# Attention and a two-layer FFN in one kernel: late attention visits at other places, the last tiles prepared earlier, and the last tile projected in two halves

## The chip, the core and the metric

The kernel runs on one core of a Trainium2 chip. The metric is the device time of one execution in microseconds (us); less is better. Engines are named as the profile names them: PE (TensorE, matmuls), PEld (its weight loads), DVE (VectorE), ACT (ScalarE), POOL (GpSimd) and SP (SyncE, which issues DMAs here).

## The reference

Local attention with a few global keys and a linear distance bias, then an FFN without biases:

```python
scores = scale * q @ k^T + bias          # (4, 8, 768, 64), bias = -slope_h * distance
keep   = (pos_k < n_global) | (0 <= rel < n_local)          # 8 and 96
a      = exp(where(keep, scores, -1e9) - max); a /= sum(a) + 1e-9
x      = (a @ v) as 3072 x 512
h      = x @ w_in                        # 512 x 2048
out    = max(0.01 * h, h) @ w_out        # 2048 x 512
```

## The kernel before

The 3072 rows of x are 24 steps of 128 rows. A step has two units of attention (four heads each), 48 in all. Attention is computed in the band alone, and at the end of it a flag tells whether that was allowed. The FFN runs in float32r with every operand cut into a high and a low part (three matmuls for one product). Most engines follow the order of the program text (`pin`, `keep_in_program_order`).

**The slots.** The first 18 steps are FFN chunks of three steps. `order` lists 6 chunks x 16 blocks of hidden features, 96 slots j. Slot j computes the hidden block (`ffn1`, `hidden`: 12 matmuls of 128x384 into `ps_h`; ACT copies it out at L1069, DVE does the leaky ReLU at L1070, ACT casts the high part gh at L1075, DVE subtracts for the low part gl at L1076) and then projects the block of the slot before (`ffn2`, `project`: 9 matmuls of 128x512 into `ps_o`). Where a chunk ends, in slots 48, 64 and 80, three sums are copied out of PSUM and stored.

**The visits.** Attention for units 22 to 47 is done two units at a time at the head of the slots in `VISITS` (`visit`): attention times v for the two units scored two visits ago, then scores for the next two, all on PE; DMA loads for the visit after (`qs`, `kr`, `vr`); ACT copies `xo` out; DVE adds the bias (L214) into one of two buffers `pr` (one for even, one for odd units); ACT exponentiates. The rest goes to `behind`, four steps taken up in this slot and the next. Its `sums` ends with a transpose on DVE and `move`: SP stores `pr` to DRAM (`via`, L239) and, when that has landed, issues four loads of `pt` from it (L241). The tiles `ps_v` hold scores and outputs in different columns.

From step 15 on, outputs go by way of DRAM (`xd`, stored by POOL's DMA queue at L363). In slot 68, `RELOAD`, one chunk's part of it is loaded (768 KB, L564); in slots 72 to 75 it is split.

**The last six tiles.** Steps 18 to 23 (768 columns of x) go through `strassen`: pairs of hidden blocks by a seven-product scheme, which needs sums s1 to s4 of weights, made on POOL (`make_sums`, ten additions, L550), and differences d1 to d4 of x blocks, made on POOL too (`diff`, L528), all of them split into high and low (`split_sum`, `split_x`: one cast on ACT, one subtraction on DVE). `prepare(n)` does this for the first pair in the last slots, n counted from the end (n = -12 is slot 84, n = -1 is slot 95); the pools of attention must be closed before (`early.close()`). `make_sums(1)` is for the second pair. In the loop of `strassen` the copy u1 (L698) is what lets the next product use the first product's bank. The sums of the six tiles are in `o`, one PSUM tile of 128x512 each; `put` copies one out and stores it (L655, L657).

Of the kernel before, what the change touches and what calls it, by code (L numbers as in the profile page):

```python
# [10 lines left out]
F32 = mybir.dt.float32  # L11
# [7 lines left out]
P = 128  # L19
# [3 lines left out]
PAIRS = 22  # L23
HT = 384
SUPER = 2 * HT // P
VISITS = [39, 42, 46, 49, 53, 56, 60, 63, 67, 70, 74, 77, 81, 84, 88]
RELOAD = 68
TB = 32
G = 8
# [24 lines left out]
def fast_path(ctx, tc, qp, kp, vp, wi, wo, nvec, weights, nmall, out, B, H, S):  # L54
    nc = tc.nc
    NB = S // P
    DM = H * D
    NK = DM // P
    NF = wi.shape[0]
    NSTEP = B * NB  # L60
    NCHUNK = len(CHUNKS)
    NPLAIN = NSTEP - SUPER
# [4 lines left out]
    wih, wil, woh, wol = weights  # L67
# [15 lines left out]
    one, fl, flag = few[:, 0:1], few[:, 1:5], few.bitcast(I32)[0:1, 5:6]  # L83
# [20 lines left out]
    def pin(ins):  # L104

        if pinned[0]:
            tc.keep_in_program_order(ins)
# [398 lines left out]
    late, here = {}, {}  # L506
# [7 lines left out]
    def value(k):  # L514
        return late[k] if k[0] == "d" else late[k][1].bitcast(F32)
# [5 lines left out]
    def split_x(k, v=None):  # L521
        v = value(k) if v is None else v
        pin(nc.scalar.copy(out=late[k][0], in_=v))
        pin(nc.vector.tensor_tensor(out=late[k][1], in0=v, in1=late[k][0].bitcast(F32), op=ALU.subtract))

    def diff(name, in0, in1):
        t = pools["mem"].tile([P, 2, HT], F32, tag="diff", name="diff", bufs=2)
        pin(nc.gpsimd.tensor_tensor(out=t, in0=value(in0), in1=value(in1), op=ALU.subtract))  # L528
        late[name] = t
# [4 lines left out]
    def blocks_of(i):  # L534
        f = 2 * i
        return dict(a11=block(i, f, 0), a12=block(i, f, 1), a21=block(i, f + 1, 0), a22=block(i, f + 1, 1))

    def make_sums(i):

        if i >= NF // 2:  # L540
            return
        b = blocks_of(i)
        a11, a12, a21, a22 = ([x.bitcast(F32) for x in b[k]] for k in ("a11", "a12", "a21", "a22"))
        for k, *terms in (("s1", a21[0], (ALU.add, a22[0]), (ALU.add, a21[1]), (ALU.add, a22[1])),
                          ("s2", here["s1"], (ALU.subtract, a11[0]), (ALU.subtract, a11[1])),
                          ("s3", a11[0], (ALU.subtract, a21[0]), (ALU.add, a11[1]), (ALU.subtract, a21[1])),
                          ("s4", a12[0], (ALU.subtract, here["s2"]), (ALU.add, a12[1]))):
            acc_ = terms[0]
            for op, t in terms[1:]:
                pin(nc.gpsimd.tensor_tensor(out=here[k], in0=acc_, in1=t, op=op))  # L550
                acc_ = here[k]

    def split_sum(i, k):
        if i >= NF // 2:
            return
        pin(nc.scalar.copy(out=late[k][0], in_=here[k]))
        pin(nc.vector.tensor_tensor(out=late[k][1], in0=here[k], in1=late[k][0].bitcast(F32), op=ALU.subtract))
# [13 lines left out]
    pools = {}  # L571

    def prepare(n):

        if n == -12:
            for k in ("b11", "b21"):
                t = xts.tile([P, 4, HT], F32R, tag="xt", name=k)
                late[k] = [t[:, :2], t[:, 2:]]
                load_x(k)
        elif n == -8:  # L580
            early.close()
            pools["mem"] = mem = phase.enter_context(tc.tile_pool(name="late", bufs=1, side="right", reuse_waits="tile"))
            pools["ps"] = phase.enter_context(tc.tile_pool(name="ps_q", bufs=1, space=bass.MemoryType.PSUM, side="right", reuse_waits="tile"))
            for k in ("b22", "t1", "t2", "t3", "t4"):
                late[k] = [mem.tile([P, 2, HT], F32R, name=k + x) for x in "hl"]
            late["b12"] = late["t3"]
            for k in ("b12", "b22"):
                load_x(k)
            for k in ("s1", "s2", "s3", "s4"):
                late[k] = [mem.tile([P, 2, P], F32R, name=k + x) for x in "hl"]  # L590
                here[k] = mem.tile([P, 2, P], F32, name=k)
            make_sums(0)
            diff("d1", "b12", "b11")
            band_holds(tc, fl, nvec, nmall)
        elif n == -7:
            band_holds_everywhere(tc, fl, pools["ps"].tile([P, HT], F32, tag="ps_p", name="ps_f")[0:1, 0:1], flag)
        elif n == -6:
            split_sum(0, "s2")
            split_sum(0, "s3")
        elif n == -5:  # L600
            split_sum(0, "s1")
            split_sum(0, "s4")
            split_x("b11")
        elif n == -4:
            diff("d2", "b22", "d1")
            split_x("t1", late["d1"])
        elif n == -3:
            split_x("t2", late["d2"])
            diff("d4", "d2", "b21")
        elif n == -2:  # L610
            split_x("t4", late["d4"])
            diff("d3", "b22", "b12")
            split_x("b21")
        elif n == -1:
            split_x("t3", late["d3"])
            split_x("b22")
            make_sums(1)

    def strassen():

# [4 lines left out]
        o = oa  # L625
# [22 lines left out]
            pin(nc.vector.tensor_tensor(out=t, in0=in0, in1=ps, op=op))  # L648
            return t

        def put(tt, bank):

            ob = (outs.tile([P, DM], F32, tag="kept", name="part", bufs=CHUNKS[0]) if tt < 3
                  else mem.tile([P, DM], F32, tag=("t2h", "t3h", "t1h")[tt - 3], name="part"))
            pin((nc.vector.tensor_copy if tt % 2 else nc.scalar.copy)(out=ob, in_=bank))  # L655
            r0 = (NPLAIN + tt) * P
            pin((nc.scalar if tt == SUPER - 1 else nc.sync).dma_start(out=out[r0:r0 + P, :], in_=ob))  # L657

        count = [0] * 6

        def second(g, n):

            i, gs = g
            (f, half_), tt = (((0, 0), (1, 1), (1, 0), (0, 1)) if i < NF // 2 - 1 else ((0, 0), (1, 0), (1, 1), (0, 1)))[n // 3], n % 3
            if len(o) < 6 and half_:
                o.extend(ps_o.tile([P, DM], F32, tag="ps_o", name="ps_o") for _ in range(3))
            gh, gl = gs[f, half_]
            to = tt + 3 * half_
            count[to] += 1
            project(tc, o[to], weights, gh, gl, tt, 2 * i + f, count[to] == 1, count[to] == NF)  # L670
            if count[to] == NF:
                put(to, o[to])

        g, rest = None, lambda: None
        for i in range(NF // 2 + 1):
# [17 lines left out]
            x, y = banks[::-1] if i % 2 else banks  # L693
            gs = {}
            ps = x()
# [22 lines left out]
            ps = x()  # L718
# [17 lines left out]
            g = i, gs  # L736
# [10 lines left out]
    ev_at.update({33: [20], 36: [21]})  # L747
    ev_at.update({j: [t] for j, t in zip(VISITS, range(PAIRS, NUNIT + 4, 2))})

# [15 lines left out]
    for j in range(len(order)):  # L765
        pinned[0] = j < half + NF or j >= VISITS[0]
        conv = list(conv_at.get(j, ()))
# [154 lines left out]
def band_holds(tc, fl, nvec, nmall):  # L922

    nc = tc.nc
    nc.vector.tensor_reduce(out=fl[:, 3:4], in_=nmall, axis=mybir.AxisListType.X, op=ALU.max)
    nc.vector.tensor_scalar(out=fl[:, 0:1], in0=nvec[:, 0:1], scalar1=float(G), scalar2=None, op0=ALU.is_le)
    nc.vector.tensor_scalar(out=fl[:, 1:2], in0=nvec[:, 1:2], scalar1=1.0, scalar2=None, op0=ALU.is_ge)
    nc.vector.tensor_scalar(out=fl[:, 2:3], in0=nvec[:, 1:2], scalar1=float(WIN + 1), scalar2=None, op0=ALU.is_le)
    nc.vector.tensor_scalar(out=fl[:, 3:4], in0=fl[:, 3:4], scalar1=9.0e8, scalar2=None, op0=ALU.is_lt)
    nc.vector.tensor_tensor(out=fl[:, 0:2], in0=fl[:, 0:2], in1=fl[:, 2:4], op=ALU.mult)  # L930
    nc.vector.tensor_tensor(out=fl[:, 0:1], in0=fl[:, 0:1], in1=fl[:, 1:2], op=ALU.mult)


def band_holds_everywhere(tc, fl, ps, flag):

    nc = tc.nc
    tc.keep_in_program_order(nc.tensor.matmul(ps, lhsT=fl[:, 0:1], rhs=fl[:, 0:1], start=True, stop=True))
    nc.vector.tensor_scalar(out=fl[0:1, 1:2], in0=ps, scalar1=P - 0.5, scalar2=None, op0=ALU.is_ge)
    nc.vector.tensor_copy(out=flag, in_=fl[0:1, 1:2])
# [139 lines left out]
    return gh, gl  # L1079


def project(tc, o, weights, gh, gl, tt, f, first, last):
    nc = tc.nc
    woh, wol = weights[2:]
    ts_ = slice(tt * P, (tt + 1) * P)
    tc.keep_in_program_order(nc.tensor.matmul(o, lhsT=gh[:, ts_], rhs=woh[:, f, :], start=first, stop=False))  # L1086
    tc.keep_in_program_order(nc.tensor.matmul(o, lhsT=gh[:, ts_], rhs=wol[:, f, :], start=False, stop=False))  # L1087
    tc.keep_in_program_order(nc.tensor.matmul(o, lhsT=gl[:, ts_], rhs=woh[:, f, :], start=False, stop=last))  # L1088


def tile_kernel(tc, a, out, B, H, S):
# [83 lines left out]
```

## Time and profile before

| | |
|---|---|
| median of 3 runs | 642.09 us (641.04 to 642.49) |
| the profiled execution | 640.23 us, its span 638.7 us |
| busy share of the span | PE 97%, PEld 85%, DVE 66%, ACT 45%, POOL 19% |
| matmuls | 5692 |
| DMA | 90.83 MB, mean 142 GB/s |

The span goes from the first to the last instruction of one profiled execution; about 1.5 us of that execution's time lies around it. A busy share is a mean over stages with different limits. Matmuls are pipelined, so that one is shown for longer than the distance to the next.

### The profile page before, as it was taken

Reading aid. Unit: us, or ns where it says so; the run is one execution under the profiler, and the core shown is the slowest. Engines: PE = TensorE matmul, PEld = TensorE weight load, DVE = VectorE, ACT = ScalarE, POOL = GpSimd, SP = SyncE. Lnnn points to the kernel's source line nnn. Section 1 sums busy time; section 2 is a strip of 40 time slices with the busy share of each in tenths; the row PEclk is TensorE's granted clock in tenths of the full one; section 3 lists DMA queues with packets and bytes.
Section 4 is the critical chain, followed back from the end, with each engine's and each line's share of the span. In section 5 each row is a group of like instructions: output and inputs, shape, how many; then the busy total and the mean of one; then the engine's idle time right before and its main releaser. Section 6 shows DMA issues by size and latency. Waiting matters only on the chain.

```text
span 638.7 us, 14739 instructions
## 1 busy us (share of the span) xinstructions
PE 616.5 (97%) x5692; PEld 543.9 (85%) x5692; DVE 419.3 (66%) x1187; ACT 288.1 (45%) x822; POOL 121.3 (19%) x160
## 2 busy tenths in 40 slices
PE   5699999999999999999999999999999999999996
PEld 4488898898888888888888888898888888888885
DVE  6988998895666466575646566666227875555543
ACT  6987755545443344454434354445223532222222
POOL 4213200000000000000010010000145765555400
PEclk8999999999999999999999999999999999999999
DMA  8976743413667345375655666665620000000002
GB/s 265 348 278 206 239 133 133 159 39 126 213 200 230 109 113 176 120 249 177 194 161 184 223 197 198 203 214 195 182 67 1 17 34 1 1 1 0 2 1 103
DMA packets 56669, 90.83 MB, mean 142 GB/s; under 512 B 10144, under 2 KB 30688, under 8 KB 56592
## 3 DMA queue, kind: packets, MB, share of 16 engines
q1 hardware_dynamic: 54944, 84.83, 40.8%
q0 software_dynamic: 1504, 4.72, 2.6%
q8 instruction: 47, 0.77, 0.5%
q14 instruction: 30, 0.25, 0.1%
q10 hardware_dynamic: 144, 0.26, 0.1%
HBM read 68.29 MB, written 21.50 MB: 141 GB/s over the span
## 4 chain that ended last, share of the span: by engine, by line
PE 87%; DVE 6%; ACT 3%; issue 2%; POOL 1%; DMA 0%; DVEq 0%; ACTq 0%; POOLq 0%
PE ps_o L1088 11%; PE ps_o L1087 11%; PE ps_o L1086 11%; PE ps_h L1065 11%; PE ps_h L1067 10%; PE ps_h L1066 10%; PE ps_p L630 9%; PE ps_v L200 2%; PE ps_v L345 2%; PE ps_q L1086 2%; PE ps_q L1088 2%; PE ps_q L1087 2%; PE ps_v L333 1%; PE ps_av L200 1%; DVE w L824 1%
## 5 line engine op out<-in xcount | busy, mean ns | idle before, releaser
L1088 PE MATMUL ps_o<-woh,gl 128*128 128x512 f32 x336 | 133.4, 397 | 0.1
L1065 PE MATMUL ps_h<-xh,wih 128*128 128x384 f32 x384 | 132.8, 346 | 0.1
L1086 PE MATMUL ps_o<-woh,gh 128*128 128x512 f32 x336 | 132.4, 394 | 0.2
L1087 PE MATMUL ps_o<-wol,gh 128*128 128x512 f32 x336 | 132.4, 394 | 0.0
L1067 PE MATMUL ps_h<-xh,wil 128*128 128x384 f32 x384 | 129.4, 337 | 0.0
L1066 PE MATMUL ps_h<-xl,wih 128*128 128x384 f32 x384 | 129.3, 337 | 0.0
L1069 ACT COPY t<-ps_h 128x384 f32<-128x384 f32 x96 | 45.7, 476 | 123.8 <-PE ps_h L1067 123.8
L1070 DVE SCALAR_TENSOR_TENSOR t<-t 128x384 f32<-128x384 f32 x96 | 59.7, 622 | 62.8 <-ACT t L1069 61.8
L363 POOL DMA_DIRECT2D xd<-xo x18 | 13.3, 738 | 372.5 <-ACT xo L362 372.5
L229 ACT ACTIVATE pr<-pr,nmall 128x168 f32<-128x168 f32 (+1 forms) x192 | 80.3, 422 | 6.4 <-DVE nmall L214 6.0
L1065 PEld LDWEIGHTS ps_h<-xh,wih 128*128 128x128 f32 x384 | 72.0, 188 | 8.4 <-issue 1.8
L1076 DVE TENSOR_TENSOR gl<-t,gh 128x384 fp32r<-128x384 f32 x96 | 54.4, 567 | 35.9 <-ACT gh L1075 35.9
L1088 PEld LDWEIGHTS ps_o<-woh,gl 128*128 128x128 f32 x336 | 63.1, 188 | 15.9 <-DVE gl L1076 1.2
L1066 PEld LDWEIGHTS ps_h<-xl,wih 128*128 128x128 f32 x384 | 72.1, 188 | 3.0
L1067 PEld LDWEIGHTS ps_h<-xh,wil 128*128 128x128 f32 x384 | 72.1, 188 | 0.1
L1086 PEld LDWEIGHTS ps_o<-woh,gh 128*128 128x128 f32 x336 | 63.1, 188 | 10.1 <-ACT gh L1075 0.8
L1087 PEld LDWEIGHTS ps_o<-wol,gh 128*128 128x128 f32 x336 | 63.1, 188 | 10.0
L1075 ACT CAST gh<-t 128x384 fp32r<-128x384 f32 x96 | 49.1, 511 | 48.6 <-DVE t L1070 47.9
L550 POOL TENSOR_TENSOR s<-s,wil 128x256 f32<-128x256 f32 x48 | 44.1, 920 | 3.8
L214 DVE CUSTOM_DVE_ANT_0 pr<-ps_v,nbw 128x168 f32<-128x168 f32 x88 | 23.2, 329 | 26.4 <-ACT xo L362 12.4
L229 ACT ACTIVATION_READ_ACCUMULATOR pr<-pr,nmall 128x1 f32 x192 | 36.5, 190 | 0.0
L256 DVE TENSOR_SCALAR pr<-pr,rs 128x168 f32<-128x168 f32 (+1 forms) x136 | 32.2, 301 | 1.0
(186 smaller groups left out, 916.1 us busy)
## 6 DMA issues: line engine op xcount, KB each, us to landing
kr<-in_kp_dram SPq DMA_DIRECT2D x40, 336.0 KB, 4.5
vr<-in_vp_dram SPq DMA_DIRECT2D x40, 320.0 KB, 5.2
via<-pr SPq DMA_DIRECT2D x30, 384.0 KB, 2.7
pt<-via SPq DMA_DIRECT2D x120, 96.0 KB, 2.4
wst<-in_wi_dram SPq DMA_DIRECT2D x16, 512.0 KB, 3.6
wst<-in_wo_dram SPq DMA_DIRECT2D x16, 512.0 KB, 3.5
qs<-in_qp_dram SPq DMA_DIRECT2D x24, 256.0 KB, 4.3
out_dram<-part SPq DMA_DIRECT2D x20, 256.0 KB, 2.5
```

The source lines that it names most:

```text
L229: pin(nc.scalar.activation(out=p, in_=p, func=AF.Exp, scale=-1.0, bias=nm[:, 2 * a + j:2 * a + j + 1], accum_out=sm[:, 2 * a + j:2 * a + j ...
L630: tc.keep_in_program_order(nc.tensor.matmul(ps, lhsT=w[x][:, m], rhs=late[k][y][:, m], start=first and m == n == 0, stop=m == 1 and n == 2 ...
L1065: tc.keep_in_program_order(nc.tensor.matmul(ps, lhsT=wih[:, k, fs], rhs=xh[:, k, :CT], start=(k == 0), stop=False))
L1066: tc.keep_in_program_order(nc.tensor.matmul(ps, lhsT=wih[:, k, fs], rhs=xl[:, k, :CT], start=False, stop=False))
L1067: tc.keep_in_program_order(nc.tensor.matmul(ps, lhsT=wil[:, k, fs], rhs=xh[:, k, :CT], start=False, stop=(k == NK - 1)))
L1069: pin(copy(out=t, in_=ps))
L1070: pin(nc.vector.scalar_tensor_tensor(out=t, in0=t, scalar=0.01, in1=t, op0=ALU.mult, op1=ALU.max))
L1075: pin(copy(out=gh, in_=t))
L1076: pin(nc.vector.tensor_tensor(out=gl, in0=t, in1=gh.bitcast(F32), op=ALU.subtract))
L1086: tc.keep_in_program_order(nc.tensor.matmul(o, lhsT=gh[:, ts_], rhs=woh[:, f, :], start=first, stop=False))
L1087: tc.keep_in_program_order(nc.tensor.matmul(o, lhsT=gh[:, ts_], rhs=wol[:, f, :], start=False, stop=False))
L1088: tc.keep_in_program_order(nc.tensor.matmul(o, lhsT=gl[:, ts_], rhs=woh[:, f, :], start=False, stop=last))
```

## The change

- `VISITS`: fifteen visits as before, the first at slot 39; the last at 84 where it was 88. Neighbours are three or four slots apart in both; there are four slots across 48, 64 and 80.
- `prepare`: what began at n = -8 (closing the pools, loading b12 and b22, the first `make_sums`, d1) and d2 are now in n = -12; the flag, the splits, d4, `make_sums(1)` and d3 are spread over n = -11 to -2, with one or two splits in each. n = -1 has none.
- `project` takes a range of columns, and the last round of the last tile (index `SUPER - 1`) is done as two halves of 256 columns; `put` then copies the left half on DVE and stores it from SP's queue, and copies the right half on ACT and stores it from ACT's queue. Before, DVE copied the whole tile and ACT's queue stored it.

```diff
-VISITS = [39, 42, 46, 49, 53, 56, 60, 63, 67, 70, 74, 77, 81, 84, 88]
+VISITS = [39, 42, 45, 49, 52, 55, 58, 61, 65, 68, 71, 74, 77, 81, 84]
...
                 load_x(k)
-        elif n == -8:
             early.close()
...
             make_sums(0)
             diff("d1", "b12", "b11")
+            diff("d2", "b22", "d1")
+        elif n == -11:
             band_holds(tc, fl, nvec, nmall)
+        elif n == -10:
+            band_holds_everywhere(tc, fl, pools["ps"].tile([P, HT], F32, tag="ps_p", name="ps_f")[0:1, 0:1], flag)
+            split_sum(0, "s2")
+        elif n == -9:
+            split_sum(0, "s3")
+            split_sum(0, "s1")
+        elif n == -8:
+            split_sum(0, "s4")
+            split_x("t1", late["d1"])
+            diff("d4", "d2", "b21")
+            make_sums(1)
         elif n == -7:
-            band_holds_everywhere(tc, fl, pools["ps"].tile([P, HT], F32, tag="ps_p", name="ps_f")[0:1, 0:1], flag)
+            split_x("t2", late["d2"])
+            diff("d3", "b22", "b12")
         elif n == -6:
-            split_sum(0, "s2")
-            split_sum(0, "s3")
+            split_x("b11")
         elif n == -5:
-            split_sum(0, "s1")
-            split_sum(0, "s4")
-            split_x("b11")
+            split_x("t4", late["d4"])
         elif n == -4:
-            diff("d2", "b22", "d1")
-            split_x("t1", late["d1"])
+            split_x("t3", late["d3"])
         elif n == -3:
-            split_x("t2", late["d2"])
-            diff("d4", "d2", "b21")
+            split_x("b21")
         elif n == -2:
-            split_x("t4", late["d4"])
-            diff("d3", "b22", "b12")
-            split_x("b21")
-        elif n == -1:
-            split_x("t3", late["d3"])
             split_x("b22")
-            make_sums(1)
...
+            if halves_:
+                for cols, copy, queue in ((slice(0, DM // 2), nc.vector.tensor_copy, nc.sync),
+                                          (slice(DM // 2, DM), nc.scalar.copy, nc.scalar)):
+                    pin(copy(out=ob[:, cols], in_=bank[:, cols]))
+                    pin(queue.dma_start(out=rows[:, cols], in_=ob[:, cols]))
+                return
...
+            if count[to] == NF and to == SUPER - 1:
+                for n, cols in enumerate((slice(0, DM // 2), slice(DM // 2, DM))):
+                    project(tc, o[to], weights, gh, gl, tt, 2 * i + f, False, True, cols, n > 0)
+                put(to, o[to], True)
+                return
```

## Rows read from the trace of the kernel before

**Rows 1.** Windows: us, busy us of each engine, clock, DMA share, GB/s.
```profile
453.00:470.00 17.00, 17.00 (x157) 15.12 (x156) 4.47 (x8) 4.52 (x10) 1.56 (x3) 1.00 0.43 112
...
504.00:521.00 17.00, 16.30 (x83) 14.19 (x81) 14.45 (x24) 8.36 (x18) 14.58 (x15) 1.00 0.13 48
```

**Rows 2.** PE's waits from 75 us to the end: total us, times, longest.
```profile
PE ps_p L630 <- ACT u L698: 0.7, 1, 0.7
```

**Rows 3.** Timeline of PE, 492 to 513 us: start, us, what.
```profile
492.50 0.39 PE L1086 MATMUL ps_o<-woh,gh 128*128 128x512 f32 x1
...
496.67 0.39 PE L1086 MATMUL ps_o<-woh,gh 128*128 128x512 f32 x1
...
505.53 0.39 PE L1088 MATMUL ps_o<-woh,gl 128*128 128x512 f32 x1
506.61 0.62 PE L630 MATMUL ps_p<-b,wih 128*128 128x384 f32 x2 [0.69 <-ACT u L698]
...
508.23 0.40 PE L1088 MATMUL ps_o<-woh,gl 128*128 128x512 f32 x1
508.65 0.44 PE L630 MATMUL ps_p<-t3h,s3h 128*128 128x384 f32 x1
...
512.42 0.34 PE L630 MATMUL ps_p<-t4h,wil 128*128 128x384 f32 x1
512.71 0.45 PE L630 MATMUL ps_p<-b22h,s4h 128*128 128x384 f32 x1
```

**Rows 4.** Timeline of ACT, at 505 us.
```profile
505.35 0.83 ACT L523 CAST b22h<-b22l 128x768 fp32r<-128x768 f32 x1
```

**Rows 5.** Timeline of DVE, 501 to 504 us.
```profile
501.65 1.49 DVE L524 TENSOR_TENSOR b<-b 128x768 fp32r<-128x768 f32 x1
503.07 1.09 DVE L1070 SCALAR_TENSOR_TENSOR t<-t 128x384 f32<-128x384 f32 x1
```

**Rows 6.** Timeline of POOL: the first and last of the first additions and differences.
```profile
473.84 0.74 POOL L550 TENSOR_TENSOR s<-wih 128x256 f32<-128x256 f32 x1
...
482.92 2.03 POOL L528 TENSOR_TENSOR diff<-t3l,b 128x768 f32<-128x768 f32 x1
```

**Rows 7.** DVE's waits, 225 to 470 us.
```profile
DVE pr L214 <- ACT xo L362: 14.6, 7, 2.4
...
DVE pr L214 <- DMA via<-pr: 3.0, 1, 3.0
```

**Rows 8.** Timeline of PE: first matmuls of the visits at 67 and 70.
```profile
363.74 0.45 PE L333 MATMUL ps_v<-pt,vr 64*64 64x128 f32 x8
...
379.19 0.45 PE L333 MATMUL ps_v<-pt,vr 64*64 64x128 f32 x8
```

**Rows 9.** Timeline of SP's DMA issues, 385 to 390 us.
```profile
385.19 1.73 SPq L241 DMA_DIRECT2D pt<-via  x4
386.96 0.43 SPq L164 DMA_DIRECT2D qs<-in_qp_dram  x1
...
388.39 0.90 SPq L182 DMA_DIRECT2D vr<-in_vp_dram  x2
```

**Rows 10.** Timeline of POOL: the reload.
```profile
372.61 0.79 POOL L564 DMA_DIRECT2D xl<-xd  x1 [4.40 <-DVE pr L256]
```

**Rows 11.** Tile vr, 386 to 398 us: its two loads.
```profile
DMA to landing us min/median/max: 6.0/6.1/6.2
```

**Rows 12.** Timeline of the end, all engines.
```profile
632.30 0.40 PE L1087 MATMUL ps_o<-wol,gh 128*128 128x512 f32 x1
...
632.54 0.40 PE L1088 MATMUL ps_o<-woh,gl 128*128 128x512 f32 x1
632.97 0.69 DVE L655 COPY part<-ps_o 128x512 f32<-128x512 f32 x1 [0.71 <-PE ps_o L1088]
633.70 0.37 ACTq L657 DMA_DIRECT2D out_dram<-part  x1
```

**Rows 13.** Line L657, the stores of the last six tiles.
```profile
DMA to landing us min/median/max: 2.0/2.9/3.9
```

More of the change, by code (lines that the diff above doesn't have):

```diff
@@ L649, in add, with put @@
             return t
-        def put(tt, bank):
+        def put(tt, bank, halves_=False):
             ob = (outs.tile([P, DM], F32, tag="kept", name="part", bufs=CHUNKS[0]) if tt < 3
                   else mem.tile([P, DM], F32, tag=("t2h", "t3h", "t1h")[tt - 3], name="part"))
+            rows = out[(NPLAIN + tt) * P:(NPLAIN + tt + 1) * P, :]
+            if halves_:
[4 more added lines that the diff above has]
+                return
             pin((nc.vector.tensor_copy if tt % 2 else nc.scalar.copy)(out=ob, in_=bank))
-            r0 = (NPLAIN + tt) * P
-            pin((nc.scalar if tt == SUPER - 1 else nc.sync).dma_start(out=out[r0:r0 + P, :], in_=ob))
+            pin(nc.sync.dma_start(out=rows, in_=ob))
         count = [0] * 6
@@ L1079, in hidden, with project @@
     return gh, gl
-def project(tc, o, weights, gh, gl, tt, f, first, last):
+def project(tc, o, weights, gh, gl, tt, f, first, last, cols=slice(None), more=False):
     nc = tc.nc
-    woh, wol = weights[2:]
+    woh, wol = (x[:, f, cols] for x in weights[2:])
     ts_ = slice(tt * P, (tt + 1) * P)
-    tc.keep_in_program_order(nc.tensor.matmul(o, lhsT=gh[:, ts_], rhs=woh[:, f, :], start=first, stop=False))
-    tc.keep_in_program_order(nc.tensor.matmul(o, lhsT=gh[:, ts_], rhs=wol[:, f, :], start=False, stop=False))
-    tc.keep_in_program_order(nc.tensor.matmul(o, lhsT=gl[:, ts_], rhs=woh[:, f, :], start=False, stop=last))
+    for g, w, start, stop in ((gh, woh, first, False), (gh, wol, False, False), (gl, woh, False, last)):
+        tc.keep_in_program_order(nc.tensor.matmul(o[:, cols], lhsT=g[:, ts_], rhs=w, start=start, stop=stop,
+                                                  skip_group_check=more))
 def tile_kernel(tc, a, out, B, H, S):
```

## The prediction

> **What bounds the kernel now.** I read the page first: TensorE (PE) is busy 97% of the span, so only time in which PE stands still can be won. The windows come next. In a stretch with little beside the FFN (453 to 470 us) PE is busy for all 17.00 us and VectorE (DVE) for 4.47; from 504 to 521 us PE loses 0.70 us while DVE has 14.45 and GpSimd (POOL) 14.58 [rows 1]. The list of PE's waits, taken from 75 us to the end, has one entry: 0.7 us for ScalarE's (ACT) copy of u1 [rows 2]. So the late visits, all before 470 us, cost PE their own matmuls and nothing else that the list shows.
>
> The matmul timeline shows how much that place really costs. A full slot takes 4.17 us (492.50 to 496.67) [rows 3]. A 128x512 matmul starts 0.24 us after the one before it [rows 12]; nine of them and twelve 128x384 ones fill a slot, so the latter are spaced by (4.17 - 9 x 0.235) / 12 = 0.17. Three pairs in the first step of the last six tiles are wider: 505.53 to 506.61 (1.08, so 0.84 lost), 508.23 to 508.65 (0.42, 0.18 lost), 512.42 to 512.71 (0.29, 0.12 lost), and the first matmul after each takes 0.1 longer than its kind (0.44 and 0.45 where 0.34 is usual) [rows 3]. Together 1.14 + 0.3 = 1.44 us.
>
> What made u1 late stands on ACT: from 505.35 it cast b22 for 0.83 us, ahead of u1's copy, which PE's matmul at 506.61 had waited for [rows 3, 4]. That cast is the last step of `prepare`; it came late because DVE was late: the splits there take 1.49 us and the 0.01-ReLU of L1070 takes 1.09 [rows 5], while POOL was doing `make_sums(1)`. Two splits, the ReLU and the subtraction of one slot are together more than a slot.
>
> After the last matmul (632.54 + 0.40 = 632.94) follow a 0.69 us copy on DVE, a DMA issue on ACT's queue at 633.70 [rows 12], and the landing: the stores of the last six tiles took 2.0 to 3.9 us for it [rows 13]. The span ends at 638.7.
>
> **The change part by part.**
>
> *The preparation.* No instruction is added or taken away: the same loads, twenty additions, four differences and splits are issued earlier. What it removes is the crowding in the last slots, hence up to 1.44 us. Whether the new places are free I work out in slots of 4.17 us. The visit at 84 is now the last, so `late` can open there. POOL's ten additions took from 473.84 to 482.92, 9.1 us or 2.2 slots, and a difference 2.03 [rows 6]. If they start a slot and a half after the loads, as in slots 88 and 89 before, s2 is made by slot 86.6, s4 by 87.7, d1 and d2 by 88.7. Their splits come behind slots 86 to 89, each after its input. d4 waits for t1's split and ends near 89.3; `make_sums(1)` runs to 91.5 (to 92.1 at the DVE-laden pace of rows 5), d3 to 92.6; t4 and t3 are wanted behind 91 and 92, that is by 92 and 93. It fits, t3 by about half a slot. On DVE the slots from 89 on hold one large split instead of two: 1.09 + 1.49 (the subtraction L1076, taken as slow as a split) + 1.49 = 4.07 of 4.17 us even with POOL always running [rows 5]. So no queue builds up, but it is close. Three DMA issues (b12, b22 behind b11, b21) and POOL's order behind the last visit's stores are hidden: nothing on PE wants them before s2. In the first step of the last tiles ACT and DVE have neither t3 nor b22 before u1, and POOL is still. I take -1.4; bounds 0 (the stall only moves) and -1.44.
>
> *The visits.* Fifteen visits stay, with the same instructions; slots 48, 64 and 80 held none before either. What changes is the spacing: seven pairs were three slots apart and seven four; now eleven and three, up to four threes in a row. Three slots and a visit are 363.74 to 379.19, 15.45 us [rows 8]. Does SP's queue keep up? Its order is loads for the next visit, then for each of two units a `via` store, a wait for its landing, and four `pt` loads. Behind the visit at 67 the second unit's store had landed only at 385.19 (its `pt` loads start then), 21.45 us after that visit; DVE, which wants that `pr` buffer for the next visit's second unit, waited 3.0 us for it [rows 7, 9], and SP could start the next loads at 386.96, 7.8 us into the visit [rows 8, 9]. PE felt almost none of it [rows 2]: DVE's 3 us are just covered by the 4.17 us between a hidden block and its projection. What had held the stores up there was the reload's 768 KB, issued at 372.61 in between [rows 10]. With three slots after three, each visit's loads start 15.45 us after the last ones, and the cycle (loads, store, `pt`, store, `pt`) is short of that away from the reload, so it holds; at 68 the reload comes again, earlier within its visit, and the three after it (71, 74, 77) inherit the lateness with no four-slot gap to recover. The v loads took 6.0 to 6.2 us to land [rows 11]; the second of two is issued at 388.9, 9.7 us after its visit began [rows 8, 9], and so lands at 15.9. With a three-slot gap PE would want them at 15.45. If lateness is as large as then, PE waits 0.4 us a visit; if it is 0.5 us smaller, nothing. Bounds 0 and, at four visits with up to 0.75 each, +3.0. I take 0 because the reload now starts before the stores instead of between them, which costs the first store more and the second less.
>
> *The last tile.* Three 128x512 matmuls become six of 128x256. A half-width one costs at least 0.12 (half of 0.24) and at most the 0.17 of a 128x384 one, so the six cost 0 to 0.3 us more; I take 0.05, nearer to proportion, since 384 to 512 columns scales so. The copy of 0.69 is cut into two of about 0.35 [rows 12]. If they ran side by side, and the first under the second half's matmuls, the store would be issued 0.34 earlier. But both halves lie in one PSUM tile. In the late visits DVE's L214 waited 14.6 us in 7 waits for ACT's copy of `xo` [rows 7], though the two only read, and other columns of that tile. So I take them in sequence: 0.35 + 0.35 and a hand-over of some 0.05, behind the last matmul, +0.1 with the matmuls. The Trainium skill's page "PSUM — Partial Sum Buffer", section "PSUM bank collisions raise a hardware error", says the same for any two engines on one bank, reads too, and asks for order by bank rather than by address; that rule, taken alone, speaks against cutting one bank's tile in two, and the waits agree with it. By it the store goes out 0.1 later, without it 0.3 earlier. The second store carries half the bytes, which helps by at most the 1.9 us between the slowest and the fastest landing [rows 13]; all six had the same size, so the row doesn't say that size made one slow, and I take 0. The part: +0.1, bounds -2.0 and +0.5.
>
> The sum: -1.4 + 0 + 0.1 = -1.3 us. Against the profiled execution, 640.23, that is 638.9. The median of the runs shown is 1.86 above that execution; against it, 642.09, the forecast is 640.8.
>
> **The rivals.** About 0.2%, 1.3 us, is what a measurement of this kernel can tell from no change; the forecast stands on that edge.
>
> *The stall moves.* POOL runs through `make_sums(1)` and d3 up to slot 92.6; if it is half a slot slower, t3's cast waits at the head of ACT's queue and FFN work stands behind it. For: DVE and POOL slow each other [rows 5, 6]. Against: 4.07 of 4.17. It would give back up to 1.0 of 1.44: 641.8.
>
> *The end gains as well.* The halves overlap, or the smaller last store lands as fast as the others: 0.3 to 1.9 on top, say 0.8: 640.0.
>
> *The visits become the bound.* Loads for a visit land after PE wants them, in the run from 65 to 77. It decides once SP's next loads start later than about 7.4 us into a visit with three slots behind it; before, the one such case was 7.8, with four slots behind it. Price 0.4 to 0.75 a visit and a growing lag: at 0.75 for four visits +3.0, less 1.3: 643.8, slower. Against: only the reload's visit was that late.
>
> *It doesn't do what it says*: preparation was never on the path. Against: the wait for u1 is PE's only one [rows 2]. It would leave 642.1, and its chance is in that of the stall that moves.
>
> **How the numbers follow.** Forecast 0.50; stall moves 0.20; end gains too 0.15; visits bound 0.15, with half of that under +2 us and so near no change. The forecast's own spread is 0.5 us on either side of 640.8, and 640.8 is itself the 0.2% line: half of it counts as faster, a little less as same. Faster: 0.27 + 0.15 + 0.03 (a small move of the stall) = 0.45. Slower by over 0.2% needs over 643.4: 0.07. Same: 0.48. The range runs from the case of the gaining end with some spread, 639.4, to the visits at half their price, 642.7.
>
> **What would show it.** Right: no wait for u1 among PE's waits, and the steps' pairs of matmuls at 0.24 and 0.17 us; b22's cast over before slot 95; POOL idle in the first step of the last tiles; DVE's copy of the last tile's first half starting only after its last matmul and ACT's after DVE's. Wrong: an idle PE at the start of a visit at 71, 74 or 77 with `vr` as the releaser, DVE's wait for `via` over 3 us; an idle PE in slots 89 to 94; a last store landing in 2 us.

## The result and the profile after

The changed kernel takes 647.79 us in the median (645.53 to 649.56, six runs), the kernel before 642.09 beside it (640.92 to 642.49, six runs): a ratio of 1.0084, interval 1.0067 to 1.0100. It is slower by 5.7 us. Forecast were 640.8, in a range of 639.4 to 642.7.

The shares of the chain that ended last, from the page of the kernel after:

```profile
PE 80%; DVE 7%; DMA 5%; ACT 3%; issue 2%; SPq 1%; POOL 1%; DVEq 0%; POOLq 0%; ACTq 0%
```

DMA stood at 0% of that chain before and PE at 87%. The windows, with the two stretches of [rows 1] and the stretch of the visits at 71, 74 and 77 (us, then busy us and count of PE, PEld, DVE, ACT, POOL, then clock, DMA share, GB/s):

```profile
453.00:470.00 17.00, 17.00 (x157) 15.15 (x157) 4.47 (x8) 4.34 (x10) 7.34 (x10) 1.00 0.37 109
504.00:521.00 17.00, 17.00 (x90) 15.80 (x89) 9.08 (x17) 6.48 (x13) 0.98 (x2) 1.00 0.12 47
...
386.00:434.00 48.00, 43.18 (x501) 36.72 (x499) 25.68 (x100) 21.10 (x72) 4.33 (x6) 1.00 0.58 184
```

The stretch at 504 us is repaired: PE 17.00 of 17.00 where it had 16.30, POOL 0.98 where it had 14.58. But from 386 to 434 us PE stands still for 4.82 us; before, it was busy for all 48.00 of them. PE's waits from 75 us on, where [rows 2] had one entry, and DVE's wait that answers to the last of [rows 7] (total us, times, longest):

```profile
PE ps_o L1100 <- ACT gh L1088: 3.4, 3, 2.1
PE ps_v L333 <- DMA vr<-in_vp_dram: 1.4, 3, 0.6
```

```profile
DVE pr L214 <- DMA via<-pr: 16.0, 5, 4.5
```

There are two sorts of stall: three visits begin late because their v loads have not landed, and three projections come late because ACT's cast of `gh` is late. The second sort is the larger. For the worst one, the timelines of DVE, ACT and PE (start us, us, what, the idle time before it):

```profile
430.37 0.33 DVE L214 CUSTOM_DVE_ANT_0 pr<-ps_v,nbw 128x168 f32<-128x168 f32 x1 [4.51 <-DMA via<-pr]
...
431.51 0.35 DVE L938 TENSOR_REDUCE few<-nmall 128x1 f32<-128x192 f32 x1
...
432.36 0.55 DVE L1083 SCALAR_TENSOR_TENSOR t<-t 128x384 f32<-128x384 f32 x1
```

```profile
432.94 0.51 ACT L1088 CAST gh<-t 128x384 fp32r<-128x384 f32 x1 [1.24 <-DVE t L1083]
```

```profile
431.03 0.34 PE L1080 MATMUL ps_h<-xh,wil 128*128 128x384 f32 x1
433.50 0.50 PE L1100 MATMUL ps_o<-woh,gh 128*128 128x512 f32 x1 [2.14 <-ACT gh L1088]
```

DVE holds the bias-and-minimum instruction of the visit's second unit until the `pr` buffer has been stored; the ReLU of the FFN slot (L1083) stands behind it in DVE's queue, ACT's cast behind the ReLU, PE's projection behind the cast. ACT is only the messenger. At this visit, the thirteenth, four small instructions of the flag (431.51 to 432.44) stand ahead of the ReLU as well, some 0.9 us. The store of that `pr` was late because SP was late. SP's DMA issues over the same stretch:

```profile
396.57 0.43 SPq L164 DMA_DIRECT2D qs<-in_qp_dram  x1
397.09 0.85 SPq L167 DMA_DIRECT2D kr<-in_kp_dram  x2
397.99 0.90 SPq L182 DMA_DIRECT2D vr<-in_vp_dram  x2
399.94 0.33 SPq L239 DMA_DIRECT2D via<-pr  x1
405.87 2.61 SPq L241 DMA_DIRECT2D pt<-via  x4
408.58 0.44 SPq L239 DMA_DIRECT2D via<-pr  x1
412.16 1.73 SPq L241 DMA_DIRECT2D pt<-via  x4
413.93 0.43 SPq L164 DMA_DIRECT2D qs<-in_qp_dram  x1
414.46 1.10 SPq L167 DMA_DIRECT2D kr<-in_kp_dram  x2
415.61 0.90 SPq L182 DMA_DIRECT2D vr<-in_vp_dram  x2
417.31 0.33 SPq L239 DMA_DIRECT2D via<-pr  x1
423.60 2.05 SPq L241 DMA_DIRECT2D pt<-via  x4
425.75 0.38 SPq L239 DMA_DIRECT2D via<-pr  x1
430.26 1.73 SPq L241 DMA_DIRECT2D pt<-via  x4
```

This is the round to learn to read. From one load of queries to the next it takes 413.93 - 396.57 = 17.36 us. A first store goes out about 1 us behind the last of the loads, and its landing releases the `pt` loads only 5.9 us after its issue (399.94 to 405.87; 417.31 to 423.60 is 6.3); the second takes 3.6 to 4.5. SP stands still in both. A visit with three slots behind it lasts 15.45 us [rows 8]: a round of this size adds some 2 us to SP's lateness. The loads of the visits at 55, 58 and 61 began 4.1, 6.2 and 8.0 us after the visit's first matmul; then a four-slot gap came. Those of 68, 71 and 74 began 4.9, 9.4 and 9.7 us after it, and PE waited at each of the visits that they delayed. The jump at 71 is the round with the reload, 19.7 us (376.89 to 396.57). At 74 little was added, since that visit itself began 17.1 us after the one at 71.

The round has no fixed size. One that began at 295.48 us took 14.80. Of this kernel's first stores between 285 and 418 us, those issued within 1.1 us of the last load landed after 4.4 to 6.3 us (7.7 with the reload beside it), those issued 1.7 us or more behind it after 2.9 to 4.0. A late SP finds its store ready and issues it right behind the loads, so lateness also lengthens the round; that is a reading of this trace and was not tested by itself. In the kernel before, the round behind the reload, which [rows 9] begins, went on so:

```profile
390.30 0.33 SPq L239 DMA_DIRECT2D via<-pr  x1
396.10 1.75 SPq L241 DMA_DIRECT2D pt<-via  x4
397.94 0.38 SPq L239 DMA_DIRECT2D via<-pr  x1
400.65 1.74 SPq L241 DMA_DIRECT2D pt<-via  x4
402.43 0.45 SPq L164 DMA_DIRECT2D qs<-in_qp_dram  x1
```

It took 402.43 - 386.96 = 15.47 us, with a four-slot gap behind the visit.

For the other two parts, the end of the kernel and the one new stall of the preparation. The end, all engines:

```profile
639.66 0.28 PE L1100 MATMUL ps_o<-woh,gl 128*128 128x256 f32 x1
639.98 0.43 DVE L661 COPY part<-ps_o 128x256 f32<-128x256 f32 x1 [0.71 <-PE ps_o L1100]
640.43 0.33 SPq L662 DMA_DIRECT2D out_dram<-part  x1
640.44 0.37 ACT L661 COPY part<-ps_o 128x256 f32<-128x256 f32 x1 [0.57 <-DVE part L661]
640.84 0.37 ACTq L662 DMA_DIRECT2D out_dram<-part  x1
```

The half-width matmuls start 0.11 to 0.12 us apart (639.08 to 639.66 for the six), half of a whole one's distance. The two copies run one after the other, and the last store is issued 0.86 us after the first copy's start, where it was 0.73 [rows 12]. From that start to the end of the span it is 5.7 us in both kernels.

The new stall, in POOL's and DVE's timelines:

```profile
475.89 1.85 POOL L528 TENSOR_TENSOR diff<-t3l,b 128x768 f32<-128x768 f32 x1
477.82 2.04 POOL L528 TENSOR_TENSOR diff<-b22l,diff 128x768 f32<-128x768 f32 x1
```

```profile
476.13 2.02 DVE L1083 SCALAR_TENSOR_TENSOR t<-t 128x384 f32<-128x384 f32 x1 [1.61 <-ACT t L1082]
478.74 1.54 DVE L1089 TENSOR_TENSOR gl<-t,gh 128x384 fp32r<-128x384 f32 x1 [0.58 <-ACT gh L1088]
```

While two differences run back to back on POOL, the slot's own two DVE instructions take 2.02 and 1.54 us where 0.55 is usual (432.36 above), and PE waits 0.4 us for `gl` at 480 us.

What adds up to the profiled difference of 645.65 - 638.69 = 6.96 us: the changed kernel reaches its first late visit 1.3 us later (227.11 against 225.79), which has nothing to do with the change (the code up to there is the same, and other runs below differ by as much); between that matmul and the last one it takes 412.55 instead of 406.75, +5.80; the end is 0.15 shorter. The +5.80 is near the +5.7 of the medians.

### The profile page after: what moved, and what is told of

It is laid out like the page before. It is cut to its first block, busy times and chain, and to the rows that moved or that the text cites. A ratio compares the mean times of both kernels' runs of the same rounds, so it can differ in the third digit from the quotient of the medians.

```text
span 645.7 us, 14757 instructions
## 1 busy us (share of the span) xinstructions
PE 619.1 (96%) x5695; PEld 545.6 (84%) x5695; DVE 417.2 (65%) x1187; ACT 289.2 (45%) x823; POOL 120.8 (19%) x160
## 4 chain that ended last, share of the span: by engine, by line
PE 80%; DVE 7%; DMA 5%; ACT 3%; issue 2%; SPq 1%; POOL 1%; DVEq 0%; POOLq 0%; ACTq 0%
PE ps_o L1100 31%; PE ps_h L1078 9%; PE ps_p L632 9%; PE ps_h L1080 9%; PE ps_h L1079 9%; PE ps_q L1100 5%; DMA via<-pr 4%; PE ps_v L200 2%; PE ps_v L345 2%; PE ps_v L333 1%; PE ps_av L200 1%; SPq L241 1%; DMA vr<-in_vp_dram 1%; DVE pr L214 1%; PE ps_tr L293 1%
## 5 line engine op out<-in xcount | busy, mean ns | idle before, releaser
L1100 PE MATMUL ps_o<-woh,gh 128*128 128x512 f32 (+1 forms) x337 | 133.0, 395 | 3.6 <-ACT gh L1088 3.4
L1100 PE MATMUL ps_o<-woh,gl 128*128 128x512 f32 (+1 forms) x337 | 134.0, 398 | 0.3
L1100 PE MATMUL ps_o<-wol,gh 128*128 128x512 f32 (+1 forms) x337 | 132.5, 393 | 0.0
L1083 DVE SCALAR_TENSOR_TENSOR t<-t 128x384 f32<-128x384 f32 x96 | 60.6, 631 | 54.6 <-ACT t L1082 53.5
L1100 PEld LDWEIGHTS ps_o<-woh,gl 128*128 128x128 f32 x337 | 63.3, 188 | 17.1 <-DVE gl L1089 2.7
```

The lines of the kernel that those rows point to most:

```text
L1083: pin(nc.vector.scalar_tensor_tensor(out=t, in0=t, scalar=0.01, in1=t, op0=ALU.mult, op1=ALU.max))
L1100: tc.keep_in_program_order(nc.tensor.matmul(o[:, cols], lhsT=g[:, ts_], rhs=w, start=start, stop=stop, skip_group_check=more))
```

## The experiments

**Theory 1.** SP is the bound of the late visits: it issues in order and stands still for each landing, its round is 17.4 us where it is late, and visits three slots apart come every 15.45. In version 1a the runs of threes alone are enough; in version 1b the reload's 768 KB at the visit at 68 is what tips it. (A three is a pair of neighbouring visits three slots apart, a four one with four slots.) **Rivals:** another part of the change is to blame (the preparation, the last tile); or the late visits are short of DMA bandwidth, so that it matters what is moved and not how it is issued; or DVE and ACT have too much to do in a three-slot gap.

The runs are read by the table at the end of this section. Its PE loss is worked out from the starts of successive matmuls, what goes beyond 0.233 us after one of 512 columns and 0.1755 after one of 384. So it counts a stall from the time at which the next matmul was due, and the slow first matmuls behind it, and comes out higher than the idle time of the windows (6.3 against 4.8 in after).

**1. The visits alone**, in the kernel before:

```
-VISITS = [39, 42, 46, 49, 53, 56, 60, 63, 67, 70, 74, 77, 81, 84, 88]
+VISITS = [39, 42, 45, 49, 52, 55, 58, 61, 65, 68, 71, 74, 77, 81, 84]
```

> The kernel before with the changed slots of the visits and nothing else. Theory 1 (SP takes one round of loads, store, wait, pt loads, store, wait, pt loads in program order; a round takes some 17.4 us, three slots and a visit 15.45): PE loses the same 6.2 us between 386 and 434 us as in the changed kernel, and the old 1.4 us before the last tiles stay, so about 6 us slower than before. Rival (the earlier preparation or the halved tile costs the time): within 1 us of before.

Measured: 649.51 us, ratio 1.0119 (1.0095 to 1.0144). PE lost 6.4 us at the visits and 2.2 around the preparation, which is in its old places here. PE's waits:

```profile
PE ps_o L1086 <- ACT gh L1075: 4.2, 3, 2.8
PE ps_v L333 <- DMA vr<-in_vp_dram: 0.8, 1, 0.8
PE ps_p L630 <- DVE u L648: 0.6, 1, 0.6
```

The visits alone make the loss, by the same two waits (the third line is the old preparation's). That another part is to blame falls.

**2. The last tile alone**, in the kernel before:

```
+    for n, cols in enumerate((slice(0, DM // 2), slice(DM // 2, DM))):
+        project(tc, o[to], weights, gh, gl, tt, 2 * i + f, False, True, cols, n > 0)
+    put(to, o[to], True)
```

> The kernel before with the last tile in two halves and nothing else. Both theories: no change, within 0.5 us; DVE's copy of the left half after the last matmul, ACT's copy after DVE's, the last store issued some 0.13 us later than before, counted from the last matmul.

Measured: 643.14 us, ratio 1.0008 (0.9997 to 1.0020). No difference that the interval can tell from none.

**3. The visits' loads on another queue**, in the kernel after: q, k and v of the next units are issued by GpSimd, the stores and `pt` loads stay with SP.

```
-                load_qk(u + 2)
+                load_qk(u + 2, nc.gpsimd)
-                load_v(u + 2)
+                load_v(u + 2, nc.gpsimd)
```

> The changed kernel with the visits' loads of q, k and v issued from POOL's queue; SP keeps the stores and loads of pt. The same bytes at about the same time. Theory 1 (SP's order is the limit): SP's round falls by the 2.3 us of issues and the loads no longer wait behind the second pt load, so they start right at each visit; PE's waits between 386 and 434 us fall from 6.2 to under 1.5, and the time to about 642. Rival 2 (the 16 DMA engines' bandwidth is the limit): the stores land as late as in the changed kernel and 5 us or more of the loss stay, about 647.

Measured: 642.80 us, ratio 1.0032 (1.0004 to 1.0060), with two of ten runs at 646.6 and 649.5. PE lost 1.15 us at the visits, in one place; PE's waits and DVE's:

```profile
PE ps_o L1100 <- ACT gh L1088: 0.8, 1, 0.8
```

```profile
DVE pr L214 <- DMA via<-pr: 5.5, 3, 3.2
```

The same bytes at the same spacing, and over four fifths of the loss are gone: bandwidth is not the bound. SP's waits for landed stores hardly changed, 76.9 us between 225 and 470 us after 79.9 in the kernel after; what left its round are the loads. The Trainium skill's page "DMA: Bandwidth & Descriptors", section "Issuing engines are not separate DMA queues", says that DMAs started from several engines end on the same DMA engines and that spreading them saves only the issue time. The run does not contradict that: the loads' issue is 2.3 us of the round here (396.57 to 398.89), and 17.4 less 2.3 is under 15.45.

**4. The same eleven threes and three fours in another order**, in the kernel after: at most two threes in a row up to 69, and a four at the reload. The five threes behind 69 cost SP less, as the last three visits load no queries and keys.

```
-VISITS = [39, 42, 45, 49, 52, 55, 58, 61, 65, 68, 71, 74, 77, 81, 84]
+VISITS = [39, 42, 45, 49, 52, 55, 59, 62, 65, 69, 72, 75, 78, 81, 84]
```

> The changed kernel with the three four-slot gaps placed elsewhere: 55 to 59, 65 to 69 (over the reload) and 42 to 45 to 49 as it is; the first and the last visit stay. Theory 1: each run of threes adds some 2 us of lag per visit and each four takes 2.2 away; with at most two threes in a row before 69 PE waits little before 75, and in all under 2 us, about 642 to 643. Rival 3 (eleven threes are too many, wherever they stand, since bytes per time decide): 5 us or more stay, about 647.

Measured: 641.41 us, ratio 0.9997 (0.9975 to 1.0018). PE lost nothing at the visits in this trace; the same list lost 1.1 and 1.2 us in experiments 6 and 7. So it is not the count of short gaps that makes the loss but where they stand. Two things were moved at once, the runs of threes and the gap at the reload; the next experiment parts them.

**5. A quarter of the reload**, in the kernel after: 192 KB are loaded at the visit at 68 instead of 768, and used four times.

```
-  pin(nc.gpsimd.dma_start(out=xt[c][1].bitcast(F32), in_=xd[:, :, :CT]))
+  pin(nc.gpsimd.dma_start(out=xt[c][1][:, 0].bitcast(F32), in_=xd[:, 0, :CT]))
```

> The changed kernel with a quarter of the reload in slot 68: 192 KB in place of 768, and that quarter of x used four times over, so three quarters of the last chunk's x are left out of the sums. Theory 1a (the run of threes alone builds up the lag): PE's waits between 386 and 434 us stay at 4 us or more of 6.2. Theory 1b (the threes only bring SP's round to the edge, where DVE still covers it, as at 58 and 61; the reload in the midst of the second run carries it over): under 2 us of them stay, time near 643.

Measured: 647.50 us, ratio 1.0081 (1.0059 to 1.0103). PE lost 6.8 us at the visits, some 1.5 of them by a lower clock (last section), and a stall appeared at 345 us as well, behind the first run of threes. Version 1b falls: the threes are enough. The reload is not free, though: SP's round with it took 17.3 us here (377.28 to 394.56) and 19.7 in the kernel after.

**6. The spaced visits alone**, in the kernel before (the list of experiment 4), to see what the new places of the preparation are worth.

> The kernel before with the spaced visits alone: its own preparation and its own last tile. The visits are free there, so PE's 1.4 to 2 us of waits around the start of the last tiles are back: the same time as before within 0.5 us, and some 1.1 us above the spaced kernel with the new preparation. If the spaced kernel owed its time to the visits and not to the preparation, this one would be as fast as it.

Measured: 643.46 us, ratio 1.0018 (1.0003 to 1.0033). PE lost 1.1 us at one visit and 2.2 around the preparation. So the visits were not free, as had been expected. Between this trace and that of experiment 4 lie 2.75 us from the first late visit to the last matmul, 1.7 of them around the preparation; the intervals of the two ratios overlap.

**7. Spaced, and the first difference between the third and the fourth sum**, in the kernel of experiment 4:

```
+            if i == 0 and k == "s3":
+                diff("d1", "b12", "b11")
...
             make_sums(0)
-            diff("d1", "b12", "b11")
             diff("d2", "b22", "d1")
```

> The spaced kernel with d1 made between s3 and s4 in place of behind s4, so that POOL's two 2 us differences no longer follow each other. Theory: the 0.4 us that are left in the preparation come from a leaky ReLU and a subtraction on DVE held by one difference each in the same slot; with short additions between them the wait goes. PE then loses nothing from the first late visit to the end of the first step, 1.5 us less than before: 640.6, a ratio of 0.9976. Rival (any POOL work in that slot holds DVE as long): 0.3 to 0.4 us stay.

Measured: 641.63 us, ratio 0.9977 (0.9963 to 0.9991): of eleven versions the one whose interval lies wholly under 1. The stall of 0.4 us became 0.24 in this trace, less of a gain than I had expected. PE lost 1.2 us at the visits all the same, mostly at 431 us.

**8. The control for experiment 3**: the same move of loads to GpSimd, in the kernel before.

> The kernel before with the visits' loads issued from POOL's queue, as a control of the same move in the changed kernel. PE hardly waits for the visits there, so nothing is to be won: within 0.5 us of before. If it is faster by 1 us or more, the move wins something that has nothing to do with dense visits; if slower, POOL's queue costs.

Measured: 642.49 us, ratio 1.0003 (0.9990 to 1.0016). With the old spacing SP's queue has nothing to give, so the gain of experiment 3 is not one of the other queue as such.

**9. The waits taken out of SP's round**, in the kernel after, visits unchanged. The four `pt` loads go behind the next visit's loads, and SP's order is the written one (the `via` stores and one load of keys are pinned for it as well):

```
-        for c in range(4):
-            nc.sync.dma_start(out=dst[c * TB:(c + 1) * TB].rearrange("p b j x -> p b (j x)"),
-                              in_=via[:, :, c].rearrange("b p x -> p b x"))
+        def back():
+            for c in range(4):
+                pin(nc.sync.dma_start(out=dst[c * TB:(c + 1) * TB].rearrange("p b j x -> p b (j x)"),
+                                      in_=via[:, :, c].rearrange("b p x -> p b x")))
...
+        if u < PAIRS:
+            back()
+        else:
+            later.append(back)
...
                 load_v(u + 2)
+        for back in later:
+            back()
+        later.clear()
```

> The kernel after, with its visits unchanged; only SP's order in the late visits is another. The four loads that bring a unit's probabilities back (pt<-via) are no longer issued right behind the unit's store, whose landing they wait for, but in the next visit, behind that visit's loads of queries, keys and values, and SP's stores, reloads and loads keep that written order. Same transfers, same bytes, same queue. Theory 1 (SP's in-order round is the bound: the two waits for a landing, some 5.8 and 2 to 4.5 us, stand in it): without these waits the round is some 2.3 us of loads, 3.5 us of the eight reloads and two stores, well under a visit with three slots; TensorE's losses at the visits fall from 6.25 us to under 0.5, and the time is the spaced version's, about 641.4 (ratio to before 0.998, between 0.996 and 1.000). Rival (the bytes and DMA traffic of the late visits, not the order of their issue, or VectorE's and ScalarE's work in a visit with three slots): same bytes and same work as in after, so the losses stay at 5 us or more and the ratio at 1.006 or above.

Measured: 642.55 us, ratio 0.9995 (0.9980 to 1.0011). SP's issues, from a stretch that answers to the one shown of after:

```profile
404.57 0.42 SPq L164 DMA_DIRECT2D qs<-in_qp_dram  x1
408.10 1.20 SPq L167 DMA_DIRECT2D kr<-in_kp_dram  x2
409.36 0.90 SPq L182 DMA_DIRECT2D vr<-in_vp_dram  x2
410.35 6.36 SPq L243 DMA_DIRECT2D pt<-via  x8
416.81 3.52 SPq L239 DMA_DIRECT2D via<-pr  x2
```

The visit at 74 begins at 405.8 here, and its v loads are out 4.5 us after that, where it was 12 in after. DVE no longer waits for `via` at all, and of the six stalls none is left; PE has one wait, of another kind, for reloaded probabilities at the visit at 71, so that it lost 1.2 us where under 0.5 was expected:

```profile
PE ps_v L341 <- DMA pt<-via: 1.2, 1, 1.2
```

That wait is a price of the edit: the eight `pt` loads were issued from 377.45 to 384.40 us, and the later ones took 6.9 to 8.0 us to land. Same bytes, same queue, same spacing, same work on DVE and ACT: only the order is another, and the old loss is gone. That DVE and ACT have too much to do falls with that of bandwidth.

**10. As 9, with the first difference placed as in 7.**

> As the run with the later reloads of the probabilities, and in the first pair's preparation the difference d1 is made between the sums s3 and s4 and no longer just ahead of d2. By theory 1 the visits lose under 0.5 us, by the theory that two differences back to back on GpSimd hold VectorE's outputs the 0.4 us at 480 us falls to 0.25 or less as it did in the spaced version: ratio to before 0.997 to 0.999, about 0.2 us under the run without this edit, which is at the edge of what is measured. Rival: the visits still lose 5 us, ratio 1.006 or more.

Measured: 642.41 us, ratio 1.0000 (0.9988 to 1.0012). PE lost nothing at the visits (120.00 of 120.00 us busy from 340 to 460) and 0.09 around the preparation, so both mechanisms did what was expected; the time did not follow by the 0.6 to 1.9 us expected.

**11. As 10, with the spaced visits.**

> As the run before it, with the late visits of the spaced list (four slots twice where the change has three). If SP's order is all that the three-slot visits suffer from, both lists give the same time here, ratio 0.997 to 0.999. If some cost of the three-slot visits is left over besides SP's order (VectorE or ScalarE late in the visit), this one is faster than the dense list by that cost, seen as stalls at the visits of the dense one.

Measured: 641.71 us, ratio 0.9989 (0.9974 to 1.0005). From the first late visit to the last matmul it differs from 10 by 0.06 us: with this order of SP's the spacing no longer matters.

In us, from the traces but for the ratio; the span is from the first matmul of the first late visit to the last matmul of the kernel:

| kernel | PE lost at visits | around preparation | first visit | visit to last matmul | ratio to before |
|---|---|---|---|---|---|
| before | 0.1 | 1.5 | 225.8 | 406.75 | 1 |
| after | 6.3 | 0.5 | 227.1 | 412.55 | 1.0084 |
| 1 visits alone | 6.4 | 2.2 | 227.5 | 414.66 | 1.0119 |
| 2 last tile alone | 0.1 | 2.1 | 228.8 | 407.41 | 1.0008 |
| 3 loads by GpSimd | 1.1 | 0.5 | 227.1 | 407.77 | 1.0032 |
| 4 spaced | 0 | 0.5 | 230.1 | 405.65 | 0.9997 |
| 5 quarter reload | 6.8 | 0.5 | 226.2 | 412.85 | 1.0081 |
| 6 spaced visits alone | 1.1 | 2.2 | 225.3 | 408.40 | 1.0018 |
| 7 spaced, difference between | 1.2 | 0.3 | 227.1 | 406.82 | 0.9977 |
| 8 control | 0 | 2.1 | 225.9 | 408.05 | 1.0003 |
| 9 later `pt` | 1.2 | 0.5 | 228.4 | 408.17 | 0.9995 |
| 10 and difference between | 0 | 0.1 | 228.3 | 406.36 | 1.0000 |
| 11 and spaced | 0 | 0.2 | 226.7 | 406.42 | 0.9989 |

In 9 the loss is the wait for `pt`. The fifth column follows the second and third, with one exception: in 3 and in 8 to 11 most of the larger visits' own matmuls take 2.81 us from the first to the FFN's next, where most take 2.70 in before and in 4. Over the fifteen visits that is 36.15 us in 10, 35.94 in 3 and 35.99 in 8 against 35.11 in before, and in 10 it eats what the preparation gave. In every visit of 2.81 us the first matmul of the scores starts before the last one of attention times v (359.67 us in 10); in those of 2.70 it starts behind it (360.96 in 4). What puts them out of step was not settled.

## Why the prediction was wrong

**The visits: the step that failed.** It said that with three slots after three "the cycle (loads, store, `pt`, store, `pt`) is short of that away from the reload, so it holds", and so put the visits at 0. The term came out at +6.2 us (6.3 lost at the visits, 0.1 before). The step had not summed the round. In the kernel before it was 15.47 us behind the reload: at the edge of 15.45, and not short of it. In the kernel after it was 17.4 where SP waited for hardly anything but landings. I took SP's queue as one that works on whatever is ready; but the `pt` loads can't be issued before a landing, and what stands behind them waits too. Experiments 3, 4 and 9 each take the loss away, or most of it, from another side (fewer items in the round, more time for it, no wait for a store's landing in it), and 5 shows that the loss comes without most of the reload. Before, the visits' mean spacing was 15.45 plus half a slot, 17.5 us, and SP still waited 43.3 us for DVE's results between 225 and 470 us (31.0 in the kernel after): lateness was worked off in each longer gap.

**The choice of 0 between 0 and +3.0** leaned on the reload's place (it "costs the first store more and the second less"). That came true, 7.7 and 2.9 us to landing where it had been 5.7 and 4.1, but the two together took longer, 10.6 us after 9.8, and the loss doesn't hang on the reload: with three quarters of it gone, 6.8 us were lost. And the bound itself was too low. It counted four late visits at up to 0.75 us, by the v loads. Those waits came as described (three, 0.4 to 0.65 us lost at each), 1.6 us together. The larger share, 0.7, 0.9 and 2.3 us, came by the path that the prediction had named and set aside: DVE's wait for `via`, "just covered by the 4.17 us between a hidden block and its projection" when it was 3.0, is not covered when it is 3.9 to 4.5. A cover has a size, and lateness that grows passes it. By an estimate from these pairs it is some 3.2 us (3.9 lost 0.7, 4.1 lost 0.9), and 0.9 less at the thirteenth visit, where the flag's instructions stand ahead of the ReLU: there 4.5 lost 2.3, and waits of 3.0 to 3.2 us lost the 0.8 to 0.9 that make up most of what is left in experiments 3, 6 and 7.

**The rival that came true** is the one in which the visits become the bound, with its mechanism, its place (71, 74, 77), its releaser and its point of decision: loads began over 7.4 us into the visits at 71 and 74, and at 61, where a four-slot gap behind it saved PE. Its price was 6.2 us instead of its +3.0. It had been given a chance of 0.15, on the ground that "only the reload's visit was that late".

**The preparation: right, and its size nearly.** The stall at the start of the products is gone. The forecast was -1.4; between the two profiles it is 1.5 - 0.5 = 1.0. The term was judged from one execution in which the old stall was small: five traces with the old places lose 1.5 to 2.2 us (mean 2.0), five with the new ones 0.5. What the text had missed is the 0.4 us at 480 us: it looked for crowding in the slots from 89 on and found room, while d1 and d2 stand back to back in slots 87 and 88, just ahead of those. Experiments 7, 10 and 11 moved d1 and brought 0.5 to between 0.1 and 0.3.

**The last tile: right.** Forecast +0.1, which no run can tell from nothing: from the first copy's start to the end it is 5.5 to 6.0 us in the nine traces with halves and 5.6 to 6.0 in the four without, and the part alone measured 1.0008, with 1 inside its interval. ACT's copy of the right half began 0.57 us late, behind DVE's copy of the left half of the same PSUM tile, as taken. That is the order by bank that the Trainium skill's page "PSUM — Partial Sum Buffer", section "PSUM bank collisions raise a hardware error", asks for; no run here shows what two copies at once would do.

**What stays open:** why the visits' matmuls of experiments 3 and 8 to 11 are 0.1 us longer; how much of the longer landings comes from the loads just ahead of a store; and whether the best of these versions, 7 at 0.9977, is better than 4 or 11, whose intervals overlap its own.

## What to carry to other kernels

Sum the round of an in-order queue before moving what feeds it: every issue and every wait for a landing that stands in it, against the shortest distance between two rounds and not the mean one. A queue behind which nothing stalls may have no room left in its tightest places; its lateness then adds up from round to round until it passes a cover that held before, so ask of each cover how many microseconds it is good for. Where such a queue stores something only to load it back, the load back belongs behind the next round's loads. Here that did at least as much as another queue for the loads (experiment 3), and fewer bytes did nothing (5); look then for a reader that now waits for the later load.

## What the runs showed of the hardware

- **The clock after a stall.** In experiment 5 PE was idle for 1.93 us, and the clock granted to it afterwards fell to its lower level, 1.2 GHz, for about 3 us: matmuls of 512 columns started 0.43 us apart instead of 0.23. That cost some 1.5 us. The windows of that kernel:

```profile
429.00:431.20 2.20, 0.40 (x3) 0.08 (x1) 1.59 (x9) 0.96 (x6) 0.00 (x0) 1.00 0.89 196
...
432.00:433.00 1.00, 1.00 (x4) 0.81 (x4) 0.96 (x5) 0.48 (x3) 0.00 (x0) 0.51 0.85 328
...
436.00:440.00 4.00, 4.00 (x22) 3.60 (x21) 3.09 (x8) 0.99 (x2) 0.00 (x0) 1.00 0.54 153
```

  The last number but two is the clock: 0.51, then 0.50, 0.50 and 0.79 in the three rows left out, then 1.00. In after, an idle time of 2.14 us at the same place left it at 1.00, as did 2.8 us in experiment 1. So such a stall may or may not cost more behind it.
- **Landing behind loads.** A store of 384 KB issued behind five loads released its waiter 5.9 to 6.3 us later, the second store of the same rounds 3.6 to 4.5 us later.
- **DVE beside POOL.** The ReLU of a slot took 2.02 us while POOL worked on differences and 0.55 without; that is more than the 1.09 of [rows 5].
- **The start of the kernel differs by run:** the first late visit began between 225.3 and 230.1 us in before, after and experiments 1 to 8, whose code up to there is the same. Two single profiles can't be compared by their spans to better than that; from one landmark to another they can.
